# Opening three quads of an attention and feed-forward kernel in a new order: gains as single rows, rows on two queues, products of zeros

## The chip, the core and the metric

The kernel runs on one core of a Trainium2 chip. A core has five engines with instruction queues of their own: TensorE (PE; its weight loads are PEld), VectorE (DVE), ScalarE (ACT), GpSimd (POOL) and SyncE (SP). DMAs are issued from the queues of SyncE and ScalarE here. Each queue is worked off in order; engines wait for one another through semaphores. The metric is device time in microseconds (us), the median of several runs.

## The reference

Two blocks in a row. With q, k, v of 8 batches, 12 heads, 448 tokens and 64 elements per head:

```
q_n = q / sqrt(mean(q*q) + 1e-6) * g_q      (the same for k with g_k)
attn = softmax(q_n @ k_n.T / 8)
x = (attn @ v), heads side by side           -> 3584 tokens x 768
h = x @ w_in                                 -> 3584 x 1024
u = h * softmax(h)
ln = (u - mean(u)) / sqrt(var(u) + 1e-6) * g_ln
out = ln @ w_out                             -> 3584 x 768
```

## The kernel before

A general path exists for inputs outside certain limits; what is timed is `fast_path`. The program holds three stages on one TensorE queue: attention for 24 "quads" (a quad is two pairs of heads), then the product with `w_in`, then the product with `w_out`. The change touches the start: what stands before the loop over quads, and quads 0, 1 and 2.

The order is written out by hand (`manual_schedule`): each helper emits its instructions where it is called, and each engine gets them in that order. `unit(...)` marks pieces of TensorE work; `later(1, f)` puts f behind the next piece.

Loads. Pairs 0 and 1 are loaded as rows (`load_rows`, line 738: four DMAs of 112 partitions per pair) because their norms and transpositions go another way than those of later pairs. Later pairs come through `load` (line 634), eight DMAs per pair, 448 KB, into five buffers. `load_v` (lines 647 and 651) loads the values of a quad by three DMAs, two buffers. Expert weights come through `load_next` (line 510), 512 KB per DMA. All but two of the row DMAs go through SyncE's queue. Each DMA takes one of eight semaphores in turn and waits until the DMA eight before it has landed.

Gains. `load_gains` loads g_q and g_k spread over 128 partitions (`gg`), the same two as rows 8 and 9 of `grow`, and the layer norm's gain as rows 0 to 7 of `grow`. `gain_columns` transposes `grow` on TensorE and copies it to `gcol` on ScalarE. Columns 0 to 7 of `gcol` are used much later, when `w_out` is prepared. Column 8 becomes g_q * g_k, times 1/8, times a flag that the gains are within limits (`gain_limit`); it scales the queries of every pair (`take_rows`, `gain`).

Norms. For rows: squares (`square_rows`), sums (`sum_rows`), inverse root (`rsqrt_seed` on ScalarE, `rsqrt_step` on VectorE), product (`normalise_rows`), transposition on TensorE (`transpose_rows`), and a copy out of PSUM (`take_rows`). For later pairs: `squares` on ScalarE (line 656), `row_sums` on VectorE (line 664), `fold_one` on VectorE or `fold_sums` on GpSimd (lines 674 and 675), the inverse root (lines 694 to 704), `normalise` on GpSimd (line 713), `qk_transpose` on VectorE (line 723), and `gain` on ScalarE (line 727).

A quad m with pairs a and b on TensorE: three score groups of a (`scores`, line 802), one group shared by both pairs (`scores_last`, line 815), three groups of b, the output products (`values_last`, line 844, and `values`, line 855), and the row sums of the exponentials (`sums`, line 874). Each score group goes into one of three PSUM banks with the tag "t" and is followed by one exponential on ScalarE (line 792). After the sums come `inverse`, `divide` (which gives `xo`) and, in the next quad, `store_x` (line 906) on SyncE's queue, with the next loads behind it.

Of the kernel before, what the change touches and what calls it, by code (L numbers as in the profile page):

```python
# [9 lines left out]
FP32 = mybir.dt.float32  # L10
# [4 lines left out]
OP = AluOpType  # L15
# [351 lines left out]
def fast_path(  # L367
# [59 lines left out]
    w_in = {k: wi.tile([P, HD, DFF // 2], FP32, name=f"w_in{k}") for k in (0, 5, 1, 4, 3, 6, 2)}  # L427
    xd = [dram.tile([DM, S], FP32, name=f"xd{b}") for b in range(B)]
    ud = [dram.tile([2, 4, 32, HF * P], FP32, name=f"ud{t}") for t in range(NT)]
    gmax = consts.tile([P, 1], FP32, name="gmax")  # L430
    within = consts.tile([P, 1], FP32, name="within")
    gcol = consts.tile([P, KF + 2], FP32, name="gcol")
    grow = work.tile([KF + 2, P], FP32, tag="tmp", name="grow")
    gg = work.tile([P, 2, D], FP32, tag="tmp", name="gg")
    mhalf = consts.tile([P, 1], FP32, name="mhalf")
    seven = consts.tile([P, 1], FP32, name="seven")
    eps = consts.tile([P, 1], FP32, name="eps")
# [24 lines left out]

    def load_gains():
        for i, g in enumerate((g_q, g_k)):
            nc.sync.dma_start(gg[:, i], g.rearrange("(o d) -> o d", o=1).to_broadcast([P, D]))
        for i, g in enumerate((g_q, g_k)):
            nc.sync.dma_start(
                grow[KF + i : KF + i + 1].rearrange("o (h d) -> o h d", h=2),
                g.rearrange("(o d) -> o () d", o=1).to_broadcast([1, 2, D]),
            )  # L470
# [6 lines left out]
    def gain_columns():  # L477
        pg = ps_t.tile([P, KF + 2], FP32, tag="t", name="pg")
        nc.tensor.transpose(pg, grow, ident[0 : KF + 2, 0 : KF + 2])
        nc.scalar.copy(gcol, pg)  # L480
        nc.gpsimd.tensor_tensor(gg[:, 0], gg[:, 0], gg[:, 1], OP.mult)

    def gain_limit():

        limit = 80.0 / float(D) ** 0.5
        nc.vector.tensor_reduce(gmax, gg[:, 0], AX, OP.max, apply_absolute_value=True)
        nc.gpsimd.tensor_scalar(large, gmax[0:1], limit, None, OP.is_gt)
        nc.vector.tensor_scalar(within, gmax, limit, float(D) ** -0.5, OP.is_le, OP.mult)

        nc.vector.tensor_scalar(  # L490
            gcol[:, KF : KF + 1], gcol[:, KF : KF + 1], gcol[:, KF + 1 : KF + 2], within, OP.mult, OP.mult
        )

# [258 lines left out]
    def sum_rows(n, s):  # L752
# [4 lines left out]
            d["ss"][:, s * 8 : s * 8 + 8], d["sq"][:, s].rearrange("p j (h d) -> p (j h) d", h=2), AX, OP.add  # L757
        )

    def normalise_rows(n, s):  # L760
        d = st[n]
        x = d["qk"][:, s].rearrange("p j (h d) -> p (j h) d", h=2)
        y = d["y"][:, s * 8 : s * 8 + 8].rearrange("p i -> p i ()").to_broadcast([R, 8, D])
        nc.vector.tensor_tensor(x, x, y, OP.mult)
# [7 lines left out]
    def take_rows(n, s):  # L772
        d = st[n]
        if s == 0:
            d["qkT"] = work.tile([P, 2, S], FP32, tag="qkT", name="qkT", bufs=3)
            nc.scalar.activation(d["qkT"][:, 0], d["pt", 0], AF.Copy, scale=gcol[:, KF : KF + 1])
        else:
            nc.vector.tensor_copy(d["qkT"][:, 1], d["pt", 1])  # L778

# [521 lines left out]
    load_rows(0, (nc.sync, nc.sync, nc.scalar, nc.scalar))  # L1301
    setup()
    load_gains()
    load_rows(1, (nc.sync, nc.sync, nc.sync, nc.sync))
    load(2)
    load_v(0)
    load(3)
    load(4)
    load(5)
    with tc.manual_schedule():  # L1310
        square_rows(0, 0, nc.vector)
        square_rows(0, 1, nc.scalar)
        sum_rows(0, 0)
        sum_rows(0, 1)
        rsqrt_seed(st[0])
        gain_columns()
        rsqrt_step(st[0])
        for s in range(2):
            normalise_rows(0, s)
            transpose_rows(0, s)  # L1320
        gain_limit()
        take_rows(0, 0)
        for s in range(2):
            square_rows(1, s, nc.scalar)
        take_rows(0, 1)
        for s in range(2):
            sum_rows(1, s)
# [2 lines left out]
        for m in range(NQ):  # L1330
# [10 lines left out]
            if m == 0:  # L1341
                unit(lambda: scores(a, 0))
                normalise_rows(1, 0)
                normalise_rows(1, 1)
                unit(lambda: scores(a, 1))
                for s in range(2):
                    transpose_rows(1, s)
                    take_rows(1, s)
                squares(2)
                row_sums(2)  # L1350
                unit(lambda: scores(a, 2))
                fold_one(2)
# [24 lines left out]
                row_sums(4)  # L1377
                unit(lambda: values(b))
                squares(5)
                unit(lambda: sums(m))  # L1380
                inverse(m)
                qk_transpose(3)
                row_sums(5)
                fold_sums(2)
                later(1, lambda m=m: divide(m))
                continue
            early = 1 < m and next1
            if early:
                rsqrt_seed(norms[m + 1])
                rsqrt_step(norms[m + 1])  # L1390
# [11 lines left out]
                    load(a + 6)  # L1402
            unit(lambda: scores(a, 1))
            if m == 1:
                gain(b)
            unit(lambda: scores(a, 2))
            unit(lambda: scores_last(m))
            if m < 2:
# [2 lines left out]
            if m == 1:  # L1411
                rsqrt_seed(norms[m + 1])
                rsqrt_step(norms[m + 1])
                normalise(a + 2)
                normalise(b + 2)
                load(a + 6)
                load(b + 6)
            unit(lambda: scores(b, 1))
            if early:
                qk_transpose(b + 2)  # L1420
                if next3:
                    load(b + 6)
# [18 lines left out]
            if scarce:  # L1441
                squares(b + 4)
                if m > 1:
                    add(b)
            if next2:
                row_sums(b + 4)
                fold_sums(m + 2)
            if not scarce:
# [13 lines left out]
                load_x(1)  # L1462
            unit(lambda: sums(m))
            inverse(m)
            if next1:
                later(1, lambda m=m: divide(m))
            if m == NQ - 2:
# [193 lines left out]
```

## Time and profile before

| | |
|---|---|
| median of 3 runs | 826.18 us (824.93 to 826.91) |
| the profiled execution | 826.51 us, of which a span of 824.4 us is in the profile |
| busy in the span | PE 796.2, DVE 673.0, POOL 462.3, ACT 461.3 us |
| DMA | 122.81 MB, mean 149 GB/s |
| attention: start of the output products of quads 0, 1, 2, 3, 4 | 19.60, 35.76, 51.81, 65.55, 78.44 us |

How to read it: a timeline line gives start and duration in us, the engine (SPq and ACTq are the queues that issue DMAs), the line of the kernel, the operation, out<-in by the program's names, the shape, and how many instructions are merged. The brackets give the idle time of the engine before it and what ended that wait. A matmul in 32-bit floats shows as two passes, so `x8` of line 802 is one score group of four matmuls. A tile's answer gives "DMA to landing", the time from issue to the arrival of the data.

### The profile page before, as it was taken

How to read it: one execution, taken by the hardware profiler on the slowest of the kernel's cores; microseconds unless marked ns; L12 is line 12 of the kernel's file. 1: busy time of each engine (PE TensorE's matmuls, PEld its weight loads, DVE VectorE, ACT ScalarE, POOL GpSimd, SP SyncE). 2: the span in 40 equal slices, each digit the busy share in tenths (PEclk: the TensorE clock that was granted, in tenths of full speed). 3: DMA queues.
4: the chain of work that ended last, by engine and by line, in shares of the span. 5: the costliest groups of instructions: out<-in, count | busy, mean ns of one | idle time of the engine just before them, and what ended most of it. 6: DMA issues, size and time to landing. Idle time of an engine off the chain costs nothing.

```text
span 824.4 us, 14924 instructions
## 1 busy us (share of the span) xinstructions
PE 796.2 (97%) x5019; PEld 465.7 (56%) x5019; DVE 673.0 (82%) x1203; ACT 461.3 (56%) x755; POOL 462.3 (56%) x635
## 2 busy tenths in 40 slices
PE   5989999999999999999999999999889999999996
PEld 3333444344443443444444444444579999999996
DVE  6769897787878888589999999998896866866945
ACT  5668777676877777255665544452424464464420
POOL 1434555455555647322254368776487777877861
PEclk9999999999999999999999999999999999999999
DMA  6677877777677663325555534452447356476312
GB/s 120 119 190 154 186 178 167 180 139 172 145 181 181 131 144 117 101 78 148 157 152 145 134 100 117 135 156 64 142 153 268 128 208 223 137 237 203 123 58 82
DMA packets 272230, 122.81 MB, mean 149 GB/s; under 512 B 190736, under 2 KB 257296, under 8 KB 272144
## 3 DMA queue, kind: packets, MB, share of 16 engines
q1 hardware_dynamic: 257888, 112.09, 51.5%
q10 hardware_dynamic: 14256, 9.67, 4.2%
q8 instruction: 42, 0.69, 0.4%
q14 instruction: 44, 0.36, 0.1%
HBM read 85.01 MB, written 36.70 MB: 148 GB/s over the span
## 4 chain that ended last, share of the span: by engine, by line
PE 76%; SPq 9%; DMA 5%; DVE 3%; POOL 3%; ACT 2%; issue 2%; ACTq 0%; DVEq 0%; POOLq 0%
PE b L972 31%; PE A L1167 14%; PE o L855 8%; PE s L802 8%; SPq L634 8%; PE B L1167 7%; PE C L1167 3%; PE sm L874 3%; DMA v<-in_v_dram 2%; PE s L815 1%; PE o L844 1%; DMA qk<-in_k_dram 1%; ACT E L792 1%; DVE part L664 1%; POOL ss L674 1%
## 5 line engine op out<-in xcount | busy, mean ns | idle before, releaser
L972 PE MATMUL b<-w_in,xg 128*128 128x512 f32 x336 | 151.2, 592 | 0.0
L792 ACT ACTIVATE E<-s 128x896 f32<-128x896 f32 x168 | 138.9, 936 | 11.9 <-PE s L802 11.2
L802 PE MATMUL s<-qkT 64*64 64x448 f32 x1152 | 123.2, 554 | 1.4 <-DVE qkT L778 0.8
L972 PE MATMUL b<-w_in,xsum 128*128 128x512 f32 x252 | 115.0, 592 | 0.0
L855 PE MATMUL o<-E,v 128*64 128x448 f32 x576 | 113.5, 543 | 0.0
L972 PEld LDWEIGHTS b<-w_in,xg 128*128 128x128 f32 x336 | 63.8, 190 | 80.2 <-issue 76.4
L674 POOL COPY ss<-part 32x56 f32<-32x56 f32 x88 | 42.0, 477 | 103.8 <-DVE part L664 101.1
L713 POOL TENSOR_TENSOR qkn<-qk,ny 128x896 f32<-128x896 f32 x46 | 77.9, 1713 | 24.3 <-DMA qk<-in_k_dram 15.9
L1167 PE MATMUL A<-w_out,sums 128*128 128x192 f32 x392 | 80.1, 327 | 3.5 <-ACT u L1179 1.6
L802 PEld LDWEIGHTS s<-qkT 64*64 64x64 f32 x1152 | 47.5, 164 | 62.1 <-ACT E L792 30.7
L972 PEld LDWEIGHTS b<-w_in,xsum 128*128 128x128 f32 x252 | 47.9, 190 | 60.3 <-issue 57.6
L1050 POOL TENSOR_TENSOR he<-he,mhalf 128x1 f32<-128x1 f32 x28 | 17.0, 608 | 114.6 <-DVE he L1049 112.5
L1167 PE MATMUL B<-w_out,sums 128*128 128x192 f32 x392 | 79.9, 326 | 1.2 <-DVE P L1211 1.2
L855 PEld LDWEIGHTS o<-E,v 128*64 128x64 f32 x576 | 39.2, 137 | 72.6 <-issue 66.8
L1056 ACT ACTIVATE u<-u,shift,he 128x1024 f32<-128x1024 f32 x28 | 34.7, 1240 | 74.6 <-POOL shift L1052 74.6
L1167 PEld LDWEIGHTS A<-w_out,sums 128*128 128x128 f32 x392 | 66.0, 190 | 4.9 <-issue 1.8
L1167 PEld LDWEIGHTS B<-w_out,sums 128*128 128x128 f32 x392 | 66.1, 190 | 1.7 <-DVE P L1211 1.5
L664 DVE TENSOR_REDUCE part<-sq 128x28 f32<-128x896 f32 x46 | 49.1, 1083 | 15.8 <-ACT sq L656 14.0
L829 DVE TENSOR_TENSOR es<-E 128x896 f32<-128x896 f32 x48 | 52.6, 1097 | 0.5 <-ACT E L792 0.5
L563 POOL TENSOR_TENSOR w_out<-w_out 128x384 f32<-128x384 f32 x44 | 50.7, 1158 | 1.9
L656 ACT ACTIVATE sq<-qk 128x896 f32<-128x896 f32 x46 | 43.9, 984 | 13.1 <-DMA qk<-in_k_dram 10.5
L723 DVE STREAM_TRANSPOSE qkT<-qkn 128x896 f32<-128x896 f32 x46 | 48.9, 1094 | 1.9 <-POOL qkn L713 1.8
(136 smaller groups left out, 1489.8 us busy)
## 6 DMA issues: line engine op xcount, KB each, us to landing
ur<-ud SPq DMA_DIRECT2D x60, 256.0 KB, 4.1
ud<-ub SPq DMA_DIRECT2D x112, 128.0 KB, 2.2
xd<-xo SPq DMA_DIRECT2D x24, 448.0 KB, 3.4
qk<-in_q_dram SPq DMA_DIRECT2D x184, 56.0 KB, 2.3
qk<-in_k_dram SPq DMA_DIRECT2D x184, 56.0 KB, 2.1
v<-in_v_dram SPq DMA_DIRECT2D x24, 384.0 KB, 4.8
out_dram<-P SPq DMA_DIRECT2D x21, 384.0 KB, 2.6
raw<-in_moe_w_in_dram SPq DMA_DIRECT2D x12, 512.0 KB, 4.8
```

What stands on the lines that cost most here:

```text
L563: nc.gpsimd.tensor_tensor(o, p, q, OP.subtract)
L634: nc.sync.dma_start(d["qk"][g * 32 : g * 32 + 32, s], src[b, h0 + g // 2].rearrange("(b t) (x d) -> x t b d", t=32, x=2)[g % 2],)
L664: nc.vector.tensor_reduce(norms[m]["part"][:, i], st[n]["sq"], AX, OP.add)
L674: e.tensor_copy(ss[g * 32 : g * 32 + 32], part[o * 32 : o * 32 + 32])
L713: e.tensor_tensor(d["qkn"], d["qk"].rearrange("p s b d -> p (s b) d"), y.rearrange("p b -> p b ()").to_broadcast([P, 2 * NB, 32]), OP.mult,)
L723: nc.vector.transpose(d["qkT"].rearrange("p s t -> p (s t)"), d["qkn"].rearrange("p b d -> p (b d)"))
L792: nc.scalar.activation(d["E", kc], s[:, :, 0:S], AF.Exp)
L802: nc.tensor.matmul(s[c : c + D, h, 0:S], d["qkT"][hh, 1, keys], d["qkT"][hh, 0, :], start=True, stop=True,)
L829: nc.vector.tensor_tensor(d["es"], d["E", 0], d["E", 1], OP.add)
L855: nc.tensor.matmul(d["o"][h * D : (h + 1) * D, :], quads[n // 2]["v"][:, n % 2 * 2 + h, kc], d["E", kc][:, h], start=False, stop=(kc == NJ ...
L972: nc.tensor.matmul(o, a[:, c], w_in[i][:, c], start=(c == 0), stop=(c == HD - 1))
L1167: nc.tensor.matmul(k[bank], a[:, c].rearrange("p a i -> p (a i)"), w_out[:, area, i, c], start=begin and c == 0, stop=c == KC - 1, skip_gr ...
```

## The change

Gains. `gg` is one partition now: g_q and g_k are loaded as single rows, multiplied there, limited there (`gain_column`), written twice side by side and turned into a column by a transposition of its own. The layer norm's gain has its own load (`load_norm_gain`, at the end of quad 0, behind the loads of pairs 6 and 7 and two weight loads) and its own transposition and copy (`norm_gain`, in quad 1 behind the second score group).

Loads. Pair 1's key rows go through ScalarE's queue, behind pair 0's; pair 3 is loaded ahead of quad 0's values.

Warm-up. Five products of zeros stand first on TensorE (`warm_up`).

Order. Pair 1's squares stand ahead of pair 0's normalisation; the key half of pair 0 is copied by ScalarE; the third score group of pair 0 stands ahead of pair 1's transpositions. In quad 0 the transposition and gain of pair 3 come ahead of the second output products; the squares and sums of pair 5 move into quad 1, behind its second score group. The norms of quad 3, which quad 2 emitted before its first score group, now come behind its second one; the row sums of pair 7 move from ahead of quad 1's output products to behind its sums.

```diff
-    gcol = consts.tile([P, KF + 2], FP32, name="gcol")
-    grow = work.tile([KF + 2, P], FP32, tag="tmp", name="grow")
-    gg = work.tile([P, 2, D], FP32, tag="tmp", name="gg")
+    gcol = consts.tile([P, KF + 1], FP32, name="gcol")
+    grow = work.tile([KF, P], FP32, tag="tmp", name="grow")
+    gg = work.tile([P, 4, D], FP32, tag="tmp", name="gg")[0:1]
...
     def load_gains():
         for i, g in enumerate((g_q, g_k)):
-            nc.sync.dma_start(gg[:, i], g.rearrange("(o d) -> o d", o=1).to_broadcast([P, D]))
...
+            nc.sync.dma_start(gg[:, i], g.rearrange("(o d) -> o d", o=1))
+
+    def load_norm_gain():
         for i in range(2):
             nc.sync.dma_start(
                 grow[i * HF : (i + 1) * HF].rearrange("c (g j) -> c g j", g=4),
...
+    def norm_gain():
+        pg = ps_t.tile([P, KF], FP32, tag="t", name="pg")
+        nc.tensor.transpose(pg, grow, ident[0:KF, 0:KF])
+        nc.scalar.copy(gcol[:, 0:KF], pg)
+
+    def gain_column():
...
+        limit = 80.0 / float(D) ** 0.5
         nc.gpsimd.tensor_tensor(gg[:, 0], gg[:, 0], gg[:, 1], OP.mult)
         nc.vector.tensor_reduce(gmax, gg[:, 0], AX, OP.max, apply_absolute_value=True)
-        nc.gpsimd.tensor_scalar(large, gmax[0:1], limit, None, OP.is_gt)
+        nc.gpsimd.tensor_scalar(large, gmax, limit, None, OP.is_gt)
         nc.vector.tensor_scalar(within, gmax, limit, float(D) ** -0.5, OP.is_le, OP.mult)
         nc.vector.tensor_scalar(
-            gcol[:, KF : KF + 1], gcol[:, KF : KF + 1], gcol[:, KF + 1 : KF + 2], within, OP.mult, OP.mult
+            gg[:, 2:4], gg[:, 0:1].to_broadcast([1, 2, D]), within, None, OP.mult
         )
+        pg = ps_t.tile([P, KF], FP32, tag="t", name="pg")[:, 0:1]
+        nc.tensor.transpose(pg, gg[:, 2:4].rearrange("o h d -> o (h d)"), ident[0:1, 0:1])
+        nc.scalar.copy(gcol[:, KF : KF + 1], pg)
...
+    def warm_up():
+
+        w = work.tile([P, 2, S], FP32, tag="r", name="warm", bufs=1)[:, 0]
+        nc.vector.memset(w, 0.0)
+        o = ps_t.tile([P, S], FP32, tag="o", name="pt", bufs=2)
+        for _ in range(5):
+            nc.tensor.matmul(o, w[:, 0:P], w, start=True, stop=True)
...
+        elif n == 0:
+            nc.scalar.copy(d["qkT"][:, 1], d["pt", 1])
...
-    load_rows(1, (nc.sync, nc.sync, nc.sync, nc.sync))
+    load_rows(1, (nc.sync, nc.sync, nc.scalar, nc.scalar))
     load(2)
+    load(3)
     load_v(0)
-    load(3)
...
+        warm_up()
...
-        gain_columns()
+        gain_column()
         rsqrt_step(st[0])
+        for s in range(2):
+            square_rows(1, s, nc.scalar)
...
-        gain_limit()
         take_rows(0, 0)
-        for s in range(2):
-            square_rows(1, s, nc.scalar)
         take_rows(0, 1)
...
                 unit(lambda: scores(a, 1))
+                unit(lambda: scores(a, 2))
                 for s in range(2):
                     transpose_rows(1, s)
                     take_rows(1, s)
                 squares(2)
                 row_sums(2)
-                unit(lambda: scores(a, 2))
...
+                qk_transpose(3)
+                gain(3)
                 unit(lambda: values(b))
-                squares(5)
                 unit(lambda: sums(m))
                 inverse(m)
-                qk_transpose(3)
-                row_sums(5)
-                fold_sums(2)
+                load_norm_gain()
                 later(1, lambda m=m: divide(m))
                 continue
-            early = 1 < m and next1
+            early = 2 < m and next1
...
             if m == 1:
-                gain(b)
+                squares(5)
+                row_sums(5)
+                fold_sums(2)
+                norm_gain()
+            if m == 2:
+                rsqrt_seed(norms[m + 1])
+                rsqrt_step(norms[m + 1])
+                normalise(a + 2)
+                normalise(b + 2)
...
+            if m == 2:
+                qk_transpose(a + 2)
+                load(a + 6)
             unit(lambda: scores(b, 1))
-            if early:
+            if early or m == 2:
                 qk_transpose(b + 2)
...
-            if next2:
+            if next2 and m > 1:
                 row_sums(b + 4)
                 fold_sums(m + 2)
...
+            if m == 1:
+                row_sums(b + 4)
+                fold_sums(m + 2)
```

More of the change, by code (lines that the diff above doesn't have):

```diff
@@ L429, in fast_path @@
     ud = [dram.tile([2, 4, 32, HF * P], FP32, name=f"ud{t}") for t in range(NT)]
-    gmax = consts.tile([P, 1], FP32, name="gmax")
-    within = consts.tile([P, 1], FP32, name="within")
-    gcol = consts.tile([P, KF + 2], FP32, name="gcol")
-    grow = work.tile([KF + 2, P], FP32, tag="tmp", name="grow")
-    gg = work.tile([P, 2, D], FP32, tag="tmp", name="gg")
+    gmax = consts.tile([P, 1], FP32, name="gmax")[0:1]
+    within = consts.tile([P, 1], FP32, name="within")[0:1]
+    gcol = consts.tile([P, KF + 1], FP32, name="gcol")
+    grow = work.tile([KF, P], FP32, tag="tmp", name="grow")
+    gg = work.tile([P, 4, D], FP32, tag="tmp", name="gg")[0:1]
     mhalf = consts.tile([P, 1], FP32, name="mhalf")
@@ L464, in load_gains @@
         for i, g in enumerate((g_q, g_k)):
-            nc.sync.dma_start(gg[:, i], g.rearrange("(o d) -> o d", o=1).to_broadcast([P, D]))
[L466 to L470, printed above, removed]
+            nc.sync.dma_start(gg[:, i], g.rearrange("(o d) -> o d", o=1))
+    def load_norm_gain():
         for i in range(2):
@@ L475, in load_gains @@
             )
[L477 to L480, printed above, removed]
+    def norm_gain():
[4 more added lines that the diff above has]
+        limit = 80.0 / float(D) ** 0.5
         nc.gpsimd.tensor_tensor(gg[:, 0], gg[:, 0], gg[:, 1], OP.mult)
-    def gain_limit():
-        limit = 80.0 / float(D) ** 0.5
         nc.vector.tensor_reduce(gmax, gg[:, 0], AX, OP.max, apply_absolute_value=True)
-        nc.gpsimd.tensor_scalar(large, gmax[0:1], limit, None, OP.is_gt)
+        nc.gpsimd.tensor_scalar(large, gmax, limit, None, OP.is_gt)
         nc.vector.tensor_scalar(within, gmax, limit, float(D) ** -0.5, OP.is_le, OP.mult)
         nc.vector.tensor_scalar(
-            gcol[:, KF : KF + 1], gcol[:, KF : KF + 1], gcol[:, KF + 1 : KF + 2], within, OP.mult, OP.mult
+            gg[:, 2:4], gg[:, 0:1].to_broadcast([1, 2, D]), within, None, OP.mult
         )
+        pg = ps_t.tile([P, KF], FP32, tag="t", name="pg")[:, 0:1]
+        nc.tensor.transpose(pg, gg[:, 2:4].rearrange("o h d -> o (h d)"), ident[0:1, 0:1])
+        nc.scalar.copy(gcol[:, KF : KF + 1], pg)
     def load_w(step):
```

## The prediction

> **What bounds the kernel now.** I read the page first (busy shares and the chain), then TensorE's timeline over the first 120 us, then the sync queue's timeline, then the answers on single tiles. Lines of "..." stand for lines left out.
>
> ```profile
> PE 796.2 (97%) x5019; PEld 465.7 (56%) x5019; DVE 673.0 (82%) x1203; ACT 461.3 (56%) x755; POOL 462.3 (56%) x635
> ...
> PE 76%; SPq 9%; DMA 5%; DVE 3%; POOL 3%; ACT 2%; issue 2%; ACTq 0%; DVEq 0%; POOLq 0%
> ```
>
> TensorE is the bound over the span; the chain leaves it mainly for the sync queue (SPq 9%). TensorE's timeline says where. A quad's output products begin with eight passes of line 844, so their starts are a clock of the quads:
>
> ```profile
> 7.88 0.25 PE L479 MATMUL pg<-ident,grow 10*128 10x10 f32 x1 [7.88 <-DMA grow<-in_moe_g_ln_dram]
> ...
> 19.60 1.01 PE L844 MATMUL o<-E,vl 64*64 64x448 f32 x8
> ...
> 31.58 0.97 PE L815 MATMUL s<-qkT 64*64 64x448 f32 x4 [1.56 <-ACT E L792]
> ...
> 35.76 1.16 PE L844 MATMUL o<-E,vl 64*64 64x448 f32 x8
> ...
> 48.55 0.98 PE L815 MATMUL s<-qkT 64*64 64x448 f32 x8 [1.65 <-ACT E L792]
> ...
> 51.81 0.93 PE L844 MATMUL o<-E,vl 64*64 64x448 f32 x8
> ```
>
> The later starts are 65.55, 78.44 and 91.34 us. Quads last 16.16, 16.05, 13.74, 12.89 and 12.90 us; 12.90 is the full-TensorE period, so what the first quads lose is 3.26 + 3.15 + 0.84 = 7.25 us. Both long waits are for exponentials on ScalarE. In quad 1 ScalarE had stood 2.35 us in the squares of pair 5, waiting for their load; in quad 2 it stood 2.68 us in the norms of pairs 6 and 7, which wait for GpSimd's fold. The edits aim at these. Behind the loads stands the sync queue:
>
> ```profile
> 34.16 1.95 SPq L634 DMA_DIRECT2D qk<-in_q_dram  x4
> 36.15 2.90 SPq L634 DMA_DIRECT2D qk<-in_k_dram  x4
> 39.15 0.90 SPq L510 DMA_DIRECT2D raw<-in_moe_w_in_dram  x2
> 40.14 0.39 SPq L647 DMA_DIRECT2D v<-in_v_dram  x1
> ```
>
> It issues a pair's load in about 0.52 us per DMA without a pause from 8.15 us (load of pair 2) to 39.15 us (first expert weights), and that is a stretch of the chain. The answer on the tile `raw` gives the landing of such weights, and that on line 802 the two speeds of one pass:
>
> ```profile
> DMA to landing us min/median/max: 4.2/4.2/6.4
> ```
> ```profile
> L802 PE MATMUL s<-qkT x96: 536/536/1007, 10.8 to 35.6; 64*64 64x448 f32 x96
> ```
>
> [...] passes of 1007 ns against 536, weight loads of four passes 0.75 us apart (11.58 and 12.33), and full speed by 15.76, some 5 us after the scores began at 10.80. [...] The second weight load, issued 0.53 us after the first, landed 2.7 us later in this trace[...].
>
> **The change, part by part.** The decisive part is one of the small ones. `grow` (the rows of the layer norm's gain) was loaded by DMAs 9 and 10 of the program and transposed at 7.88 us, before TensorE had anything else. Now `load_norm_gain` stands at the end of quad 0 and `norm_gain` after the second score group of quad 1. On the sync queue 62 DMAs come first: 6 small ones and rows, six pairs x 8 = 48, two value loads x 3 = 6, two weight loads. On TensorE the transposition comes after eight score matmuls of quad 1, and everything later waits behind it.
>
> When do the rows land? Pair 2's load moves up: the sync queue loses the broadcast and doubled gain rows, both norm-gain loads and two key-row DMAs; it issues two short gain rows (1.70 to 2.67), the first query rows of pair 1, then waits for the first row DMA's landing (below 4.18, when VectorE starts on those rows). So pair 2 starts at 4.1 instead of 8.15. From there to the weights it is the same 54 DMAs, in another order, which took 39.15 - 8.15 = 31.0 us: weights at 35.1, gain rows at 36.1 to 37.0. [...] before, these landed 4.2 and, counted from the first issue, 6.9 us after 39.15 (with values behind them). I take 5.9: the rows land at T = 41.0. Bounds: 38.0, if they pass the weights and land 1 us after their issue ends; 43, if they share with the values as the second weights did.
>
> When would TensorE be there? First scores at about 11 (below), output products near 18.5, 7.45 us of products and sums (43.54 - 35.76 = 7.8 with fill), two score groups of 0.8: about 27.5. So TensorE stands 13.5 us, as does ScalarE, whose copy of `gcol` stands ahead of five exponentials. All other engines run out of work before T.
>
> From T to quad 1's output products: 0.3 for the transposition, then five score groups. At full clock ScalarE paces them (0.82 us per exponential: 5.75 us for seven): 4.25 us, start 45.3. [...] eight passes cost 1.5 us instead of 0.8 until it has been busy some 5 us: three groups at 1.5, two at 0.8, so 6.4: start 47.4. Against 35.76 that is +11.6 us.
>
> What comes back: in quad 2 the norms stand behind two exponentials and their loads are long there. Sums end, VectorE's inverse (0.75), row sums of pair 7 (1.09), GpSimd's fold (1.3), norms (0.6): the third exponential starts 4.0 us after the sums, not 2.5, a hold-up of about 1.1 on a period of 12.9: 14.0 against 16.05, -2.0. In quad 3 VectorE is later than before (divide 2.6 us after those row sums, two transpositions, two additions, two row sums), so the next norms come 0.5 later after the sums than before: +0.5. Sum at the fourth quad: +10.1.
>
> A second return: periods above 12.90 stand in before at quad 6 (0.27), quad 10 (1.87), quad 16 (0.83) and quad 18 (0.69), 3.66 us together; the chain goes through the sync queue and late loads ahead of quad 10. In quad 3 the store of x is issued 3.4 us after the output products start (68.98 against 65.55); in the changed kernel the sync queue stays nearly where it was while TensorE is 10 us later, bounded by the division that the store waits for, so loads gain some 4 us. I take 2.8 of the 3.66, at both ends 0 and 3.66. Result: +11.6 - 2.0 + 0.5 - 2.8 = +7.3.
>
> The other edits are costed at nothing, for one reason: they end before T. The cover is 13.5 us. Without it they would be worth: the warm-up, about 1.6 us off the first 16 score passes (3.27 against 1.6); the removed wait for the broadcast gains (landing 5.0 and 5.3 us) some 4 us earlier loads; the gains' three small VectorE operations ahead of the norm step +0.35; the key half's copy on ScalarE +0.6 there; warm-up products up to five x 1.49 us cold, ending at 8.5 at worst, when the first transposition is due; the memset (no row; below the 0.62 of a VectorE copy of that size) lies under the rows' load; the second queue holds ScalarE's sequencer to about 4.6, against squares at 4.54 before, +0.1; values of quad 0 issued at 12.4 as before. All lie in front of quad 1.
>
> The profiled execution took 826.51 us with a span of 824.4, so 2.1 lie outside; I apply the sum to the median, 826.18: 833.5 us, span about 831.4.
>
> **Rivals.** (A) As above, some of the later stalls gone: 833.5, own range 830 to 836.5. Chance 0.60. (B) No return downstream, or the rows land at 43: +10.1 gives 836.3, with two more 838.3. For it: the stall ahead of quad 10 also passes VectorE (0.71 us for `es`). Against: loads do gain slack. Chance 0.20; I name 837. (C) The clock is not lost or the rows land near 38: -2.1 or -3.0 gives 831.4 or 830.5, both with full return 828: 829.5. For it: a four-partition DMA may pass the weights. Chance 0.12. (D) Not slower: the rows come early enough for the returns to outweigh the wait. At full clock quad 1's output products start 4.25 after T, so the balance 4.25 + T - 35.76 - 2.0 + 0.5 is zero at T = 33, and with 2.8 returned at T = 35.8. Against: 62 issues at the shortest common 0.48 us from 0.72 are 30.5, plus 1.9 for the shortest landing; 33 to 36 needs the queue almost without a pause, the rows past the weights and no loss of clock. With T = 33 it gives 823.4. Chance 0.08, of which 0.05 ends faster. That the change moves nothing is excluded: both programs' queues differ from the third DMA on.
>
> **How the numbers follow.** About 0.2% (1.65 us) is what a measurement of this kernel tells from no change. Faster 0.05; within 0.03; slower 0.92 (A, B, C). The range drops D and the far end of B: 828.0 to 838.5.
>
> **What would show it.** TensorE's largest wait in the changed profile: some 13 us ended by the landing of `grow`, near 41 us; score passes of about 1 us after it; output products at 19 or before, then near 47.4, 61.4, 75.6; the stall ahead of quad 10 shorter. Early loads right: pair 2 from 4.1. Wrong, if `grow` lands by 33, if TensorE finds other work, or if the wait reappears as less slack elsewhere so that quad 4 is more than 12 or less than 6 us later than 78.44.

## The result, and the profile after

| | before | changed |
|---|---|---|
| median (runs) | 826.54 us (6) | 830.68 us (6) |
| lowest, highest | 823.0, 827.9 | 830.15, 831.46 |
| profiled execution, its span | 826.51, 824.4 | 830.15, 827.9 |
| ratio, 95% interval | | 1.0056 (1.0035 to 1.0077) |

The changed kernel is slower by 4.1 us; 833.5 was forecast, with a range of 828.0 to 838.5. The interval lies clear of 1.

The page of the changed kernel, busy shares and chain:

```profile
PE 800.3 (97%) x5030; PEld 471.0 (57%) x5030; DVE 671.0 (81%) x1203; ACT 460.8 (56%) x757; POOL 463.8 (56%) x635
...
PE 88%; DVE 4%; SPq 2%; POOL 2%; DMA 2%; issue 1%; ACT 0%; DVEq 0%; POOLq 0%
```

The sync queue's share of the chain fell from 9% to 2%, and yet the kernel is longer. The chain now stays on TensorE (76% before, 88% now), with one hole. TensorE's timeline shows it (start, duration, engine, line, operation, shape, count; in brackets the idle time before and what ended it):

```profile
17.60 1.17 PE L854 MATMUL o<-E,vl 64*64 64x448 f32 x8
...
39.99 0.24 PE L476 MATMUL pg<-ident,grow 8*128 8x8 f32 x1 [12.05 <-DMA grow<-in_moe_g_ln_dram]
40.16 1.77 PE L812 MATMUL s<-qkT 64*64 64x448 f32 x8
...
45.83 0.92 PE L854 MATMUL o<-E,vl 64*64 64x448 f32 x8
...
58.33 1.82 PE L812 MATMUL s<-qkT 64*64 64x448 f32 x16 [0.93 <-ACT E L802]
59.97 0.93 PE L854 MATMUL o<-E,vl 64*64 64x448 f32 x8
```

Line 476 is the transposition of the layer norm's gain. It stood 12.05 us for its rows, with the rest of quad 1 behind it. The eight score passes after it took 1.77 us, where eight took 0.98 before (line 815 at 48.55): TensorE's granted clock was 0.50 from 30.28 to 43.94 us, with 1.00 on both sides of that stretch. What all waited for is needed much later; the answer on the tile `gcol` has the first use of these columns at 350.3 us (count, shortest, median and longest in ns, first and last start in us):

```profile
L547 ACT ACTIVATE w_out<-tmp,gcol x16: 614/615/618, 350.3 to 471.1; 128x384 f32<-128x384 f32 x16
```

The table of stretches has the means of that clock. Its columns are the stretch in us, its length, the busy time of PE, PEld, DVE, ACT and POOL (with the number of instructions), the granted clock (1.00 is full speed), the DMA share and GB/s:

```profile
0.00:30.00 30.00, 24.64 (x171) 11.36 (x171) 19.70 (x49) 16.64 (x29) 6.09 (x21) 1.00 0.72 136
30.00:45.00 15.00, 5.01 (x33) 1.98 (x37) 4.74 (x8) 4.93 (x8) 2.76 (x9) 0.54 0.80 196
45.00:60.00 15.00, 14.07 (x144) 5.66 (x140) 9.83 (x18) 10.45 (x17) 6.34 (x12) 1.00 0.41 93
```

From 30 to 45 us TensorE was busy 5.01 of 15 us at a clock of 0.54. The sync queue shows why the rows were so late: they were issued at the end of a long row of loads, with hardly a pause before them.

```profile
34.22 0.90 SPq L510 DMA_DIRECT2D raw<-in_moe_w_in_dram  x2
35.17 0.67 SPq L469 DMA_DIRECT2D grow<-in_moe_g_ln_dram  x2
35.93 0.40 SPq L647 DMA_DIRECT2D v<-in_v_dram  x1
```

The starts of the output products side by side, and how far the changed kernel is behind:

| quad | 0 | 1 | 2 | 3 | 4 | 10 | 23 |
|---|---|---|---|---|---|---|---|
| before | 19.60 | 35.76 | 51.81 | 65.55 | 78.44 | 158.08 | 326.62 |
| changed | 17.60 | 45.83 | 59.97 | 73.76 | 86.66 | 164.04 | 331.07 |
| later by | -2.00 | 10.07 | 8.16 | 8.21 | 8.22 | 5.96 | 4.45 |

From quad 4 on every period of the changed kernel is 12.90 us; before, stalls of 3.7 us in all stood between the starts of quads 5 and 18.

### The profile page after: what moved, and what is told of

It reads as the page before. It is cut to its first block, busy times and chain, and to the rows that moved or that the text cites. A ratio compares the mean times of both kernels' runs of the same rounds, so it can differ in the third digit from the quotient of the medians.

```text
span 827.9 us, 14945 instructions
## 1 busy us (share of the span) xinstructions
PE 800.3 (97%) x5030; PEld 471.0 (57%) x5030; DVE 671.0 (81%) x1203; ACT 460.8 (56%) x757; POOL 463.8 (56%) x635
## 4 chain that ended last, share of the span: by engine, by line
PE 88%; DVE 4%; SPq 2%; POOL 2%; DMA 2%; issue 1%; ACT 0%; DVEq 0%; POOLq 0%
PE b L982 31%; PE A L1177 14%; PE o L865 12%; PE s L812 12%; PE B L1177 7%; PE sm L884 5%; PE C L1177 3%; PE s L825 2%; PE o L854 2%; SPq L634 2%; DMA grow<-in_moe_g_ln_dram 1%; DVE part L664 0%; POOL sums L1156 0%; DMA x<-in_k_dram 0%; POOL qkn L713 0%
## 5 line engine op out<-in xcount | busy, mean ns | idle before, releaser
L1177 PE MATMUL A<-w_out,s 128*128 128x192 f32 x224 | 46.3, 330 | 0.6 <-ACT u L1189 0.6
```

The source lines that it names most:

```text
L1177: nc.tensor.matmul(k[bank], a[:, c].rearrange("p a i -> p (a i)"), w_out[:, area, i, c], start=begin and c == 0, stop=c == KC - 1, skip_gr ...
```

## The experiments

Two questions: does the late load make the whole loss, and do the other edits, uncovered, do what the prediction credited them with? "The column" is line 476 of the changed kernel; "early rows" is the first experiment's kernel, on which later ones build. The experiments ran on three chips, on which the kernel before took 825.69 us (first four), 826.01 (next four) and 825.42 (last three) in the median; each ratio is to the kernel before on the same chip. Differences between medians of different chips are good to about 1 us. The code cuts show the lines that matter: against the changed kernel in the first three and in "All moves together", against the kernel before in "A late TensorE" and "Late gain alone", and otherwise against the kernel that the text names. Tile declarations and the helper `keep_busy` are left out.

**Early rows.** The loads of the gain's rows go behind the values of quad 0, 21 us earlier in the queue; the column stays in quad 1.

```diff
     load_v(0)
+    load_norm_gain()
     load(4)
...
                 inverse(m)
-                load_norm_gain()
```

> The changed kernel with one move: the layer norm's gain rows are loaded behind the values of quad 0 (DMAs 26 and 27 of the sync queue) and not behind the weights; the transposition stays in quad 1. Theory W (all of the loss is TensorE's wait for these rows): the 12.05 us wait on the transposition is gone, output products of quad 1 near 35 us instead of 45.83 (ScalarE, held by pair 3's gain, sets them: its first exponential of quad 1 started at 29.96), quads 2 and 3 keep their 14.1 and 13.8, so quad 3 begins its output products near 63, 2.4 us ahead of the kernel before; 824.5 us, between 822.5 and 826.5. Rival R (the reordering itself costs, the wait only hides it): quads 2 and 3 take 16 us again, 828 us or more. Theory S (the loads of the sync queue follow TensorE with little slack): the longer periods of quads 6, 10, 16 and 18 come back, 2 to 5 us together.

Measured: 822.41 us (821.69 to 822.77), ratio to before 0.9959 (0.9944 to 0.9975). TensorE's timeline of this kernel:

```profile
29.33 0.22 PE L476 MATMUL pg<-ident,grow 8*128 8x8 f32 x1 [1.76 <-DVE r L895]
30.54 1.01 PE L812 MATMUL s<-qkT 64*64 64x448 f32 x8 [0.98 <-ACT E L802]
...
34.70 0.93 PE L854 MATMUL o<-E,vl 64*64 64x448 f32 x8
...
51.20 0.93 PE L854 MATMUL o<-E,vl 64*64 64x448 f32 x8
```

The 12.05 us have become 1.76 us (the column waits for a PSUM bank that VectorE's inverse, line 895, frees). So the place of that load costs 830.68 - 822.41 = 8.3 us (8.0 by the two ratios), twice the loss, and the rest of the change gains 3.3 over the 825.69 of the same chip. The time is a little below the 822.5 to 826.5 expected: the stalls of theory S did not come in this execution, and rival R was right about quad 2, not about the time. Quad 2 lasts 16.50 us here, where it lasted 14.14 in the changed kernel. The prediction had credited the new order with the 2 us of quad 2. Without the wait the new order alone doesn't give them.

**Late column.** The load stays late, and the column moves to quad 2, where the rows are long there.

```diff
                 fold_sums(2)
-                norm_gain()
             if m == 2:
+                norm_gain()
```

> The changed kernel with one move on the other side of the wait: the gain rows are loaded where they were, behind the weights, and their transposition and copy go from quad 1 to the same place in quad 2 (after its second score group). Theory W: the rows landed at 39.99 us and TensorE comes there after 43 us, so nothing waits; quad 1 near 35 us, 824.5 us as with the early load, within 1 us of it. If TensorE still stood some microseconds in quad 1, something else than the rows was what it waited for, and W falls: 828 us or more.

Measured: 821.53 us (821.35 to 825.54), ratio 0.9948 (0.9931 to 0.9965). The late load itself is harmless; what cost the time is that a transposition was placed ahead of its data, with all later work of TensorE behind it. The 825.54 is the profiled execution, with 3.4 us of stalls in quads 11 to 20, which the other five, all within 0.7 us of one another and some 4 us below it, can hardly have had: such stalls come and go between executions.

**Kept busy.** The wait stays, and 14 products of 128x128 by 128x448 that nothing reads run in it, so that TensorE has work until the rows come.

```diff
+                keep_busy(a, 14)
                 norm_gain()
```

> The changed kernel with 14 products of pair 2's own queries and keys (128x128 by 448, 0.747 us each at full clock, 10.5 us in all, result unused) put into the 12.05 us of waiting, ahead of the transposition. Theory C (a part of the loss is the halved clock after the wait): the score groups after the rows' landing take 0.8 us and not 1.5, the output products of quad 1 start 4.25 us after the landing and not 5.84, 1.6 us earlier, and the time falls from 830.7 to about 829.1. Rival: ScalarE's exponentials pace these groups anyway, so less than 0.5 us is gained: 830.3 or more.

Measured: 828.93 us (828.26 to 829.63), ratio 1.0043 (1.0026 to 1.0060). TensorE's timeline of this kernel:

```profile
29.26 10.79 PE L772 MATMUL hot<-qkT 128*128 128x448 f32 x28 [1.76 <-DVE r L901]
39.99 0.22 PE L476 MATMUL pg<-ident,grow 8*128 8x8 f32 x1
40.14 1.01 PE L818 MATMUL s<-qkT 64*64 64x448 f32 x8
...
43.98 0.93 PE L860 MATMUL o<-E,vl 64*64 64x448 f32 x8
```

The granted clock from 30 to 45 us is 1.00, in the changed kernel 0.54. The column runs at 39.99 us as there, the eight passes after it take 1.01 us instead of 1.77, and the output products follow 3.99 us later instead of 5.84. The clock's share of the loss is 1.85 us in this trace. In the medians it is 1.75, by the two ratios 1.1, with intervals that overlap.

**A late TensorE.** Before, with 13 unused products in quad 3 behind its second score group: is a late start partly given back?

```diff
             unit(lambda: scores(a, 1))
+            if m == 3:
+                keep_busy(a, 13)
```

> The kernel before with 13 unused products of 0.747 us (9.7 us of TensorE work at full clock) behind the second score group of quad 3, so TensorE is late by a plain delay of 9.7 us and nothing else is touched. Theory S (later stalls come from loads that have too little lead, and a late TensorE gives them lead): the longer periods of quads 6, 10, 16 and 18 (0.27, 1.87, 0.83, 0.69 us) vanish, and the time rises by 9.7 - 3.7 = 6.0, to 832.5. Rival (the stalls have causes of their own, the changed order took them away): the periods stay and the time rises by 9.7, to 836.2.

Measured: 832.62 us (832.04 to 833.13), ratio 1.0085 (1.0065 to 1.0106). The period of quad 3 grew by 9.32 us, all later ones are 12.90, and the time grew by 6.9 over that chip's median of before (825.69). In this execution the stalls of before are gone when TensorE is delayed.

**Late gain alone.** Before, in its old order, with the gain's rows loaded at the end of quad 0 and transposed in quad 1, by themselves.

```diff
                 fold_sums(2)
+                load_norm_gain()
...
             if m == 1:
                 gain(b)
+                norm_gain()
```

> The kernel before with one edit only, the suspected cause alone: the rows of the layer norm's gain are loaded at the end of quad 0, behind the weights, and transposed behind the second score group of quad 1; everything else stays in the old order. If this alone makes the wait, TensorE stands in quad 1 for the landing of the rows, issued near 39.3 us and landing 4.8 later near 44.1, and with the clock halved the output products of quad 1 start near 49.9 us (35.76 before). Theory L: quad 2 took 14.1 instead of 16.05 us in the changed kernel because ScalarE, VectorE and GpSimd worked ahead during the wait; then it is about 14 here too, in the old order of norms, output products of quad 2 near 64, and with the 3.7 us of later stalls returned the time is 825.7 + 8.5 = 834.2 us. Rival R: the other order of the norms made quad 2 short; then quad 2 stays at 16 here, and the time is 836.2. If the late rows are not the cause, the output products of quad 1 stay near 36 and the time at 826.

Measured: 837.21 us (834.67 to 837.99), ratio 1.016 (1.013 to 1.0191). TensorE's timeline of this kernel:

```profile
43.29 0.24 PE L488 MATMUL pn<-ident,nrow 8*128 8x8 f32 x1 [14.21 <-DMA nrow<-in_moe_g_ln_dram]
...
48.72 0.92 PE L852 MATMUL o<-E,vl 64*64 64x448 f32 x8
...
61.34 0.98 PE L823 MATMUL s<-qkT 64*64 64x448 f32 x8 [1.65 <-ACT E L800]
...
64.59 0.93 PE L852 MATMUL o<-E,vl 64*64 64x448 f32 x8
```

The one edit makes a wait of 14.21 us and costs more than the whole change. Quad 2 keeps 15.88 us and the same wait of 1.65 for an exponential as before (line 815 at 48.55 in the prediction). Theory L falls: the wait by itself doesn't shorten quad 2. Rival R held. The profiled execution is the quickest of the four; it got 3.8 us back after quad 3, and what makes the other three 2.2 to 3.3 us longer isn't in its trace and stays open. Two of them were granted a lower clock (0.985 against 0.989), the third was not (0.990).

**Pair 3's gain back.** Early rows, and ScalarE's scaling of pair 3 behind the second exponential of quad 1, as before had it.

```diff
                 qk_transpose(3)
-                gain(3)
...
             if m == 1:
+                gain(b)
                 squares(5)
```

> The kernel with early gain rows, and the scaling of pair 3's queries (gain) moved back behind the second exponential of quad 1, so that the first exponential isn't held by it (29.59 us with it ahead, score group done near 28). Theory F: quad 2's 16.5 us come from the fold of pair 5's sums on GpSimd, which was moved into quad 1 and ends at 36.6 us there, with ScalarE waiting 2.0 us for it; the gain's place doesn't touch that chain, so quad 1's output products come 1 us earlier (33.7 against 34.70), quad 2's at 51.2 as before, time within 0.6 us of 822.4. Rival G: the held exponential sets the pace of both quads; then quad 2's output products come 1.2 us earlier, 50.0, and the time is 821.2.

Measured: 822.44 us (821.27 to 825.97), ratio 0.9969 (0.9955 to 0.9982). Output products of quad 1 at 33.40 (1.3 sooner), of quad 2 at 51.51 (0.3 later). What was gained in quad 1 was lost in quad 2, as theory F has it. ScalarE's timeline of this kernel shows the wait for pair 5's fold:

```profile
36.94 0.34 ACT L694 ACTIVATE ny<-ss,eps 128x56 f32<-128x56 f32 x1 [3.63 <-POOL ss L675]
```

With early rows alone the same wait was 2.02 us and ended at 36.64: ScalarE was free sooner, but the fold came no sooner.

**Pair 5 back.** Early rows, and the squares, row sums and fold of pair 5 back in quad 0.

```diff
                 unit(lambda: values(b))
+                squares(5)
                 unit(lambda: sums(m))
                 inverse(m)
+                row_sums(5)
+                fold_sums(2)
...
-                squares(5)
-                row_sums(5)
-                fold_sums(2)
                 norm_gain()
```

> The kernel with early gain rows, and squares, row sums and fold of pair 5 put back into quad 0 as in the kernel before. Theory F: ScalarE no longer waits 2.0 us for the fold in quad 1; squares now stand ahead of quad 1's exponentials (+0.7 there), so its output products come near 35.4 (34.70 with them in quad 1), but quad 2 falls from 16.50 to about 14.1, output products near 49.5 against 51.20, time 820.7 us. Rival G: quad 2 stays at 16 to 16.5 and the time rises by the 0.7 to 823.1.

Measured: 822.69 us (821.17 to 826.86), ratio 0.9972 (0.9959 to 0.9984). Quad 2 lasts 14.09 us, as theory F has it. ScalarE's timelines show what was moved; first that of the kernel with early rows alone:

```profile
36.64 0.34 ACT L694 ACTIVATE ny<-ss,eps 128x56 f32<-128x56 f32 x1 [2.02 <-POOL ss L675]
37.02 0.25 ACT L695 ACTIVATE ny<-ny 128x56 f32<-128x56 f32 x1
37.17 1.71 ACT L802 ACTIVATE E<-s 128x896 f32<-128x896 f32 x2
```

and that of this kernel:

```profile
38.65 0.33 ACT L694 ACTIVATE ny<-ss,eps 128x56 f32<-128x56 f32 x1
39.01 0.25 ACT L695 ACTIVATE ny<-ny 128x56 f32<-128x56 f32 x1
39.17 1.71 ACT L802 ACTIVATE E<-s 128x896 f32<-128x896 f32 x2
```

With pair 5's fold in quad 1, line 694 waits 2.02 us for GpSimd (line 675), and the last two exponentials of quad 1 start 2.47 us after that quad's output products (37.17 - 34.70); with the fold in quad 0 they start 0.28 us before them (39.17 against 39.45). What quad 2 needs from ScalarE stands behind them. The time was not the 820.7 expected: in this execution quad 0 was already 1.8 us later (last section), pair 5's squares held the first exponentials by 0.8, and TensorE's clock was halved from 31.51 to 38.34 us (mean from 30 to 45 us 0.77; it had waited 1.76 us up to 30.96 and waited 1.82 up to 33.01), so that the output products of quad 1 began at 39.45, not 35.4. Quads 0 and 1 lost 4.75 us here, quad 2 gained 2.41. How much the other runs lost isn't shown: this execution was granted the lowest clock of the 22 (0.991, median 0.994). And a part of quad 2's gain can come from the late quad 1, which gives cover as the long wait did. The next kernel, whose quad 1 isn't late, settles most of that.

**All moves together.** Early rows, the column in quad 2, pair 3's gain and pair 5 back.

```diff
+    load_norm_gain()
     load(4)
...
-                gain(3)
                 unit(lambda: values(b))
+                squares(5)
                 unit(lambda: sums(m))
                 inverse(m)
-                load_norm_gain()
+                row_sums(5)
+                fold_sums(2)
...
             if m == 1:
-                squares(5)
-                row_sums(5)
-                fold_sums(2)
-                norm_gain()
+                gain(b)
             if m == 2:
+                norm_gain()
```

> Early gain rows, their transposition in quad 2, pair 3's gain back behind quad 1's second exponential, and pair 5's squares, sums and fold back in quad 0: all moves together. Theory F: quad 1's output products near 34, quad 2's near 48.3 (14.3), time 819.5 us. Rival G, by which only the held exponential counts: 821.2. If the moves cancel, 822.4 as with early rows alone.

Measured: 825.72 us (822.8 to 826.76), ratio 1.0 (0.9983 to 1.0016): a miss by over 6 us. It is quicker through the first quads than all kernels above (output products of quads 2 and 3 at 48.60 and 62.71, with early rows alone 51.20 and 64.90), and yet its time is that of the kernel before. Quad 2 lasts 15.28 us with output products of quad 1 at 33.32; with pair 3's gain back it lasted 18.12 from 33.40. So pair 5's move is worth 2.8 us here without a late quad 1 (the column moved too), but it doesn't bring 14.1. From quad 3 to quad 23 it takes 262.4 us, early rows alone 257.3. The chain of waits of this kernel names the largest stall, ahead of the output products of quad 10 (start, duration, what ran or was waited for):

```profile
140.73 1.51 SPq L634
...
142.81 3.04 DMA qk<-in_k_dram
...
145.88 0.96 ACT sq L656
...
146.86 1.10 DVE part L664
...
150.74 0.31 POOL ss L675
...
151.08 0.35 ACT ny L694
...
151.60 0.91 ACT E L802
...
152.56 0.98 PE s L825 x8
```

A pair's keys, issued at the sync queue's own pace, land at 145.85; squares, row sums, fold, norm and one exponential stand behind them, and TensorE behind that. The chain of before has the same links in the same place (keys waited for from 145.88 to 148.00, score group at 154.83).

**The same with a delay.** Three unused products, 2.2 us, in quad 3 of that kernel.

```diff
             unit(lambda: scores(a, 1))
+            if m == 3:
+                keep_busy(a, 3)
```

> The kernel with all moves together, plus three products of 128x128 by 448 in quad 3 whose result isn't used (0.75 us each, 2.2 us on TensorE). That kernel was at the output products of quad 3 at 62.71 us, ahead of the one with early rows alone (64.90), yet took 825.7 against 822.4: from there on it lost 5.1 us in stalls in quads 9 to 19. Theory S: these stalls are loads that arrive late because TensorE is too early for the sync queue, so TensorE's extra 2.2 us come back or more than come back: output products of quad 3 at 64.9, fewer stalls after it, time 822.5 to 825.7. Rival T: the stalls belong to the order of that kernel and stay; then the time is 827.9.

Measured: 823.91 us (820.35 to 826.75, 22 runs), ratio 0.9977 (0.9961 to 0.9992). More work made it no slower; nine of the 22 runs lie at 820.35 to 821.55, below every run of the kernel without the delay (822.8 and more, on a chip where the kernel before takes 0.6 us longer). In the profiled execution (822.9) quad 3's output products start at 65.70 and every later period is 12.90. The time is what theory S expected, with the caution that the runs scatter over 6 us, so that the stalls can't be gone in all of them.

**The old first loads.** Early rows, but the gain rows are loaded a second time as before had them, into tiles that nothing reads, and pair 1's keys go through the sync queue.

```diff
             nc.sync.dma_start(gg[:, i], g.rearrange("(o d) -> o d", o=1))
+        for i, g in enumerate((g_q, g_k)):
+            nc.sync.dma_start(gspare[:, i], g.rearrange("(o d) -> o d", o=1).to_broadcast([P, D]))
...
-    load_rows(1, (nc.sync, nc.sync, nc.scalar, nc.scalar))
+    load_rows(1, (nc.sync, nc.sync, nc.sync, nc.sync))
```

> The kernel with early gain rows and with the first loads of the kernel before: the two gain rows are loaded a second time over 128 partitions and twice side by side into tiles that nothing reads, and pair 1's key rows go through the sync queue. Pair 2's load then starts near 8.8 us instead of 3.8. Theory H: what makes the kernel with early rows faster than the one before is this lead of the loads, not the shorter first quads (its quad 2 starts only 0.6 us sooner than before's); then stalls come back between quads 6 and 18 and in the squares of pair 5, and the time is 825.5 to 827 us. Rival K: the other order pays for it, and the time stays near 822.4 to 823.2.

Measured: 825.82 us (822.42 to 829.39), ratio 1.0003 (0.9989 to 1.0018). The gain of the early rows is gone. The sync queue's line of pair 2's first load:

```profile
6.82 2.29 SPq L643 DMA_DIRECT2D qk<-in_q_dram  x4
```

It starts at 6.82 us instead of 3.76. In the profiled execution (828.83, at the upper end) quad 3's output products are 2.3 us later than with early rows alone, and from there to quad 23 it takes 262.7 us instead of 257.3. Theory H's time came: with the old first loads the gain over before is gone. How much of it is the lead of the loads, and how much came by the later first quads (this execution also lost the zeros' effect, last section), isn't separated. The granted clock doesn't sort these runs: the seven with 0.997 or more lie anywhere from 822.42 to 828.89.

**No zeros.** Early rows without the five products of zeros.

```diff
-        warm_up()
```

> The kernel with early gain rows, without the five products of zeros. They bring the full clock before the first scores; without them the first 16 score passes cost 3.27 us instead of 1.6, so quad 0's output products should start 1.6 us later than 17.22, near 18.8, and quad 1's near 36.3. Theory P: nothing later makes up for it in a kernel that has no stalls from quad 3 on, and the time is 822.4 + 1.6 = 824.0 us. Rival Q: quads 1 and 2 are paced by GpSimd's folds and by loads, so that the loss is absorbed there: 822.4 to 822.8.

Measured: 825.2 us (824.36 to 826.06), ratio 0.9993 (0.9979 to 1.0007). TensorE's timeline of this kernel at the first scores:

```profile
10.60 3.83 PE L812 MATMUL s<-qkT 64*64 64x448 f32 x24 [0.62 <-ACT qkT L786]
```

and that of the changed kernel:

```profile
10.54 2.52 PE L812 MATMUL s<-qkT 64*64 64x448 f32 x24 [0.62 <-ACT qkT L786]
```

The same 24 passes take 3.83 us without the zeros and 2.52 with them. Output products of quads 0 to 3 are 1.7 us later throughout; another 2.4 us went in stalls after quad 9 in that execution. Theory P's 1.6 us is right for the first quads, and the median moved by 2.8. The stalls are a warning for theory S: the loads of this kernel are no later than with early rows alone (first weights issued at 34.38 us against 35.36) and TensorE is later, so the loads have more lead, and still there are stalls. The lead at the start alone doesn't decide.

## Why the prediction was right

The mechanism was the one forecast: the time lost is TensorE's wait for the late rows, at a place where nothing else could run. Before showed no later work of TensorE held behind such a wait (nothing was due behind line 479); in the changed trace TensorE ran nothing from 27.94 to 39.99 us. Late rows alone make the wait (late gain alone), and taking away either the late load or the early column removes it (early rows, late column). Most of the sizes held too:

| step, in the prediction's order | forecast | measured |
|---|---|---|
| pair 2's load starts | 4.1 | 3.83 |
| first weights issued | 35.1 | 34.22 |
| gain rows issued | 36.1 to 37.0 | 35.17 to 35.84 |
| TensorE stands from, for | 27.5, 13.5 us | 27.94, 12.05 us |
| rows landed, T | 41.0 | 39.99 |
| T to output products of quad 1 | 6.4 | 5.84 |
| quad 1 later by | 11.6 | 10.07 |
| quad 2 | 14.0 | 14.14 |
| quad 3 | 14.2 | 13.79 |
| sum at quad 4 | 10.1 | 8.22 |
| returned from there to quad 23 | 2.8 | 3.77 |
| result | +7.3 | +4.1 (medians), +3.6 (profiled) |

The loss was over-estimated by 3.2 us in the medians. In the two spans, 3.5 us apart, the 3.8 us too much split into three terms. The sum at quad 4 was 1.9 too high: T by 1.0, because the queue was 0.9 us ahead of the plan at the weights; the stretch at half clock by 0.6; quad 3 by 0.4; less 0.1 that quad 2 took more. The return was 1.0 larger: all of the 3.7 us of stalls, not 2.8. And 1.0 came after quad 23, where the sum had nothing: from there to the end of the span took 496.8 us instead of 497.8. Pass by pass, the changed kernel is 4.46 us behind through all of the product with `w_in`, and again at 602 us of before, early in the product with `w_out`. In between it waited less (2.6 us between 584 and 604 us against 4.5), but then ran at half clock (0.50) from 596.89 to 600.31 us, and the two cancel. At 609 us TensorE waited 0.59 us for a sum on GpSimd before and not in the changed kernel; from 616 us on the lag is 3.76, and the last 0.3 us fall behind TensorE's last product.

Two errors ahead of the wait cancelled by luck: quad 0's output products came at 17.60 us and not near 18.5, but from there to the next scores it took 8.58 us and not 7.45, so TensorE stood from 27.94, near the forecast 27.5. Neither enters the result, which hangs on T. Rival C's sum is slightly off in the text: with both terms and the full return it gives 827.5, not 828.

The 5.9 us from the first weights' issue to the rows' landing, on which T rests, was the author's estimate between two landings of before, 4.2 and 6.9; measured, the transposition began 5.77 us after that issue (39.99 - 34.22). The rows didn't land behind both weight loads: the first landed at 38.5 us, 4.3 after its issue, the second at 40.5, 5.8 after its issue at 34.75.

On the clock: the prediction's "some 5 us" to full speed was the author's reading of one start of before (10.80 to 15.58). In the changed trace TensorE was halved at 30.28, 2.34 us after its work ended at 27.94, and full again at 43.94, 3.95 us after it began again at 39.99. The half-speed stretch is 13.65 us and the full-speed one before it, from 6.39, 23.89; the half-speed stretch from 596.89 us is 3.41, and the other two are four and seven times that. Why the clock changes when it does isn't shown.

One right number had an incomplete reason. The prediction gave quad 2 its 14 us because the norms of quad 3 stand behind two exponentials and their loads are long there. The order is needed: the old order with the same wait keeps 15.88. It isn't enough: the new order without the wait takes 16.50, and 14.09 once pair 5's squares, sums and fold go back to quad 0. So the change also moved a fold into quad 1 that costs quad 2 2.4 us in that pair of traces (2.8 in the pair of "All moves together"), and the wait covered it: GpSimd folded from 34.78 to 36.98 us, while TensorE stood. The prediction priced "the other edits" at nothing under a cover of 13.5 us and listed what several would cost without it; this one was not on the list.

The return was right in kind: all periods of the changed kernel from quad 4 on are 12.90. The chain of before at the largest stall leads back to keys that land late for TensorE, and in that kernel a delay alone removed the 3.7 us. Early loads alone don't do so reliably: without a delay the traces from quad 3 on have none with early rows, pair 3's gain back and pair 5 back, but 3.4 us with the late column, 2.4 without the zeros and 5.1 with all moves. In the changed kernel both act, and what its early loads are worth beside the delay isn't separated.

Of the rivals, B (no return) fell. C's figure, 829.5, is nearer to the time than A's 833.5, but its mechanism didn't happen: the clock was lost for 13.65 us, and the rows came at 39.99, not 38. D fell with T at 39.99, far from its 35.8. The forecast of what would show it (a wait of some 13 us ended by `grow` near 41, passes of 1 us after it) was met but for sizes; "the stall ahead of quad 10 shorter" is a period of 12.90 in place of 14.77.

Five versions are quicker than both kernels with an interval clear of 1. The two simplest are the changed kernel with the column in quad 2 (821.53, 0.9948 of before, interval 0.9931 to 0.9965) or with early rows (822.41).

## What to carry to other kernels

A small load at the end of a long queue can become the longest wait of a kernel if an instruction that uses it stands early on an engine whose later work stands behind it (here TensorE, 12.05 us, for rows issued at 35.17 us behind 62 DMAs and used 4.82 us later): count the issues ahead of it, multiply by the issue time, add the time to landing, and place the consumer after that, here one quad later. When a wait hides other edits, price each of them without it, since the next version removes the cover. And before shortening the start of a pipeline, ask whether compute or the load queue sets the pace later on: here 2.2 us of useless products cost nothing, while taking 3 us of head start from the loads went with 3.4 us in the medians, a part of which can be the later first quads.

## What the runs showed of the hardware

Products of zeros count for the clock: TensorE was granted the full clock at 6.39 us with them in the changed kernel, at 13.35 and 15.58 us in the kernels without. But the effect isn't certain. In two executions (pair 5 back, old first loads) the zeros had brought it by 4.21 and 5.11 us, it was halved again from 11.03 and 11.94 us for 3.41 us, and the head start was gone: the first 24 score passes took 4.15 and 4.04 us (2.52 in the changed kernel), output products of quad 0 at 19.00 and 19.79 instead of 17.2 to 17.9. The length of the gaps doesn't decide it alone. In pair 5 back TensorE stood 0.25, 1.23 and 0.62 us between the zeros and the first scores; in kept busy it stood 1.23 and 0.62 us there and kept the clock (the 24 passes took 2.52 us). What decides it isn't shown.

How far one program's time scatters differs from kernel to kernel. Before, with stalls for loads in its trace, six runs span 4.9 us (823.0 to 827.9); the changed kernel, with none from quad 4 on, spans 1.3 (830.15 to 831.46), and the one with early rows 1.1. But late gain alone, with none in its trace either, spans 3.3 in four runs, and the kernel with all moves and the delay 6.4 in 22. So the stalls are one source of the scatter at most; the others aren't shown.
